# Attention weights of two units of the second batch turned through DRAM by VectorE, first batch's sums of v on GpSimd

## The chip, the cores and the metric

The kernel runs on one core of a Trainium2 chip. In the profile the core's engines are PE (TensorE, matrix products and transposes by product), DVE (VectorE), ACT (ScalarE), POOL (GpSimd) and SP (SyncE, which here only issues DMA transfers, one after the other). The metric is the device time of one execution in microseconds (us). The profiled execution has a time of its own and a span, from its first to its last instruction; all times inside the program are counted from the span's start.

## The reference

Eight batches of eight heads are attended in two ways and added; the sum is the input of a two-layer network. Cut to what is computed:

```python
# q, k, v: 8 batches, 8 heads, 576 positions, 64 wide
q_d = q.reshape(B, H, 144, 4, D).mean(axis=3)      # same for k_d, v_d
out_d = softmax(scale * q_d @ k_d.T) @ v_d         # 144 pooled positions
out_up = np.repeat(out_d, 4, axis=2)
mask = np.abs(pos[:, None] - pos[None, :]) < 4
scores = np.where(mask, scale * q @ k.T, -1e9)     # 7 keys for a query
out_local = softmax(scores) @ v
x = (out_up + out_local)                           # 4608 tokens x 512
h = x @ w_in                                       # 512 x 2048
g = h * np.clip(h + 3, 0, 6) / 6
return g @ w_out                                   # 2048 x 512
```

## The kernel before

**The large products.** The network is computed over chunks of tokens: 512 in chunk 0, 256 in chunk 1, then 384 each. For 16 slices f of the inner width `gemm1` (L934) makes h in PSUM, ScalarE and VectorE gate it (L940, L944) and split it into a rounded high part (L948) and a remainder, its low half (L952), and `gemm2` (L986) adds the slice to the output. Each float32 product is three products of rounded halves. The weights come as raw words, one block per slice of w_in and of w_out (SP, L169), and each block is made into two halves by ScalarE (L180, L195, L201), VectorE (L185, L189) and VectorE or GpSimd (L205, the remainder). All this happens while chunk 0 is worked on; the halves then stay.

**Attention.** A unit is a pair of heads of one batch, so each batch has four (0 to 3). A unit has pooled q and k (L331 and L333 on GpSimd), pooled v (sums of four rows), pooled scores (`scores_d`, L428), their softmax (normalised in L492 with 432 columns), local scores in windows (L607 puts the mask in by a product, L615 the scores) and their softmax (L492 with 640 columns). The normalised weights have the queries on the partitions, and the products with v need the keys there, so the weights have to be turned.

There are two ways to turn them. Units of batches 0 and 1 (`alone = b < ALONE`, ALONE = 2) are turned by TensorE: `trans_d` (L501, two groups of three transposes) and `trans` (L638, three and two), each with a copy out of PSUM behind it. Units of later batches go by DRAM: SP writes the pooled weights out (`put_d`, L511 to L516) and reads them back in blocks of 32 by 32 (`get_d`, L522 and L527), the local ones the same (`put` L541, `get` L548), and VectorE turns each block (`turn_d` L536, `turn_l` L555). The pooled product is `pv_d` (L586; L589 for batch 0) in the first case and `pv_d4` (L570) in the second; the local product is `pv` (L656).

**Sums of v.** `ld4` (L362 for the first 512 rows, g = 0; L364 or L367 for the last 64, g = 1) loads v for pooling. `sum_pe` sums four rows on TensorE: for g = 0 by four products with the identity (L393), for g = 1 by one product with a matrix of ones (L391). `sum4` does it with one reduction on VectorE (L376) or two additions on GpSimd (L378, L379). Batch 0 uses `sum_pe` for both, batch 1 for g = 1, all others `sum4`.

**What sets the order.** Nothing is ordered by hand. Every piece of work is an `op` with an engine (or several to choose from), a cost in us, the ops it follows, the buffers it takes and frees, and for some a due time. The class `Plan` simulates the five engines with these costs and always starts the ready op with the earliest due time; the order that comes out is emitted, and each engine runs its instructions in that order. `need`, with SLACK by batch, sets the due time of a batch's units. In the time up to the first `gemm1` the planner also puts fillers on TensorE (`busy`, L1038, products of an identity without use), as many as fit in the gaps that it expects. The names of buffers in the orders below: `early`, `arena` and `rows` are places in SBUF, `a_`, `o_` and `h_` with a number are banks of PSUM, `pd_` and `pl_` are tensors in DRAM for pooled and local weights, `rawp_` is a raw weight block.

## Time and profile before

| | us |
|---|---|
| median of 3 runs | 946.02 (945.36 to 947.41) |
| profiled execution | 944.02 |
| its span | 942.2 |
| TensorE busy | 931.6 (99% of the span) |
| VectorE busy | 554.2 (59%) |
| ScalarE busy | 363.2 (39%) |
| GpSimd busy | 298.8 (32%) |

Busy is the time in which an engine works on an instruction; shares are means over a program whose first sixth (attention of the first batches, the weights, chunk 0) is unlike the rest. TensorE's granted clock is 1.00 throughout. A timeline row gives start, duration (us), engine, line, operation, result and operands with their partitions and columns, and the number of records; in brackets stands the idle time before it and what ended it. A row of groups gives busy time in us and mean nanoseconds, then idle time and what released it. A row of waits gives the engine and what it waited for, then the total, the number and the longest. A row of windows gives start and end, length, and busy time and records of PE, PEld (weight loads), DVE, ACT and POOL, then clock, DMA share and GB/s. Some float32 products show two records per instruction.

### The profile page before, as it was taken

Reading aid. Unit: us, or ns where it says so; the run is one execution under the profiler, and the core shown is the slowest. Engines: PE = TensorE matmul, PEld = TensorE weight load, DVE = VectorE, ACT = ScalarE, POOL = GpSimd, SP = SyncE. Lnnn points to the kernel's source line nnn. Section 1 sums busy time; section 2 is a strip of 40 time slices with the busy share of each in tenths; the row PEclk is TensorE's granted clock in tenths of the full one; section 3 lists DMA queues with packets and bytes.
Section 4 is the critical chain, followed back from the end, with each engine's and each line's share of the span. In section 5 each row is a group of like instructions: output and inputs, shape, how many; then the busy total and the mean of one; then the engine's idle time right before and its main releaser. Section 6 shows DMA issues by size and latency. Waiting matters only on the chain.

```text
span 942.2 us, 19819 instructions
## 1 busy us (share of the span) xinstructions
PE 931.6 (99%) x7567; PEld 808.5 (86%) x7567; DVE 554.2 (59%) x1045; ACT 363.2 (39%) x899; POOL 298.8 (32%) x386
## 2 busy tenths in 40 slices
PE   8999999999999999999999999999999999999997
PEld 5677778988889898889889888988988988998996
DVE  7888886477677566554456667555455654323322
ACT  5787755334333334333233333333233432221222
POOL 4345361244462334332325244225125320000000
PEclk9999999999999999999999999999999999999999
DMA  7999353355666565545135555645154520100101
GB/s 210 228 293 288 72 118 64 70 105 119 126 134 132 104 117 113 100 84 114 34 80 122 102 104 102 134 98 97 40 99 80 115 55 12 34 1 2 33 1 33
DMA packets 311758, 93.52 MB, mean 99 GB/s; under 512 B 251376, under 2 KB 297840, under 8 KB 311664
## 3 DMA queue, kind: packets, MB, share of 16 engines
q1 hardware_dynamic: 311376, 91.83, 43.8%
q8 instruction: 59, 0.97, 0.4%
q10 hardware_dynamic: 288, 0.43, 0.2%
q14 instruction: 35, 0.29, 0.1%
HBM read 69.60 MB, written 22.61 MB: 98 GB/s over the span
## 4 chain that ended last, share of the span: by engine, by line
PE 90%; SPq 4%; DMA 3%; DVE 1%; issue 1%; ACT 1%; POOL 0%; DVEq 0%; ACTq 0%
PE h L934 40%; PE o L986 39%; PE a L656 2%; PE a L615 2%; PE a L442 1%; PE a L986 1%; PE a L570 1%; SPq L311 1%; DMA rows<-in_k_dram 1%; DMA arena<-in_v_dram 1%; SPq L548 1%; PE a L428 1%; SPq L522 1%; SPq L527 1%; DMA arena<-in_q_dram 0%
## 5 line engine op out<-in xcount | busy, mean ns | idle before, releaser
L934 PE MATMUL h<-rounded,wp 128*128 128x384 f32 (+2 forms) x2240 | 420.1, 336 | 0.2 <-DVE arena L944 0.2
L986 PE MATMUL o<-wp,rounded 128*128 128x512 f32 x1680 | 408.1, 394 | 0.0
L934 PEld LDWEIGHTS h<-rounded,wp 128*128 128x128 f32 x2240 | 384.1, 188 | 15.1 <-issue 2.7
L986 PEld LDWEIGHTS o<-wp,rounded 128*128 128x128 f32 x1680 | 311.0, 188 | 66.1 <-issue 4.4
L940 ACT ACTIVATE arena<-h 128x384 f32<-128x384 f32 (+2 forms) x192 | 93.7, 490 | 365.6 <-PE h L934 364.7
L944 DVE SCALAR_TENSOR_TENSOR arena<-arena,h 128x384 f32<-128x384 f32 (+2 forms) x192 | 105.1, 547 | 183.0 <-ACT arena L940 181.8
L948 ACT CAST rounded<-arena 128x384 fp32r<-128x384 f32 (+2 forms) x192 | 98.2, 512 | 119.2 <-DVE arena L944 118.7
L952 DVE TENSOR_TENSOR rounded<-arena,rounded 128x384 fp32r<-128x384 f32 (+2 forms) x136 | 79.9, 588 | 78.3 <-PE o L986 42.9
L952 POOL TENSOR_TENSOR rounded<-arena,rounded 128x384 fp32r<-128x384 f32 (+2 forms) x56 | 62.5, 1118 | 156.3 <-ACT rounded L948 102.9
L331 POOL TENSOR_TENSOR arena<-arena 128x144 f32<-128x144 f32 x36 | 16.2, 450 | 182.6 <-PE a L442 101.5
L318 DVE STREAM_TRANSPOSE arena<-arena 128x576 f32<-128x576 f32 x56 | 43.1, 772 | 24.1 <-PE a L615 11.4
L492 POOL TENSOR_TENSOR arena<-arena 128x640 f32<-128x640 f32 (+1 forms) x34 | 41.7, 1227 | 20.0 <-DVE arena L485 15.9
L333 POOL TENSOR_TENSOR arena<-arena 128x144 f32<-128x144 f32 x72 | 41.1, 570 | 5.6
L837 POOL TENSOR_TENSOR rounded<-arena,rounded 128x384 fp32r<-128x384 f32 (+1 forms) x10 | 15.0, 1511 | 71.2 <-ACT rounded L120 70.9
L473 POOL TENSOR_TENSOR arena<-arena 128x640 f32<-128x640 f32 x21 | 26.5, 1264 | 27.7 <-DVE arena L470 17.1
L376 DVE TENSOR_REDUCE arena<-arena 128x128 f32<-128x512 f32 (+1 forms) x28 | 30.0, 1071 | 8.8 <-PE a L570 6.9
L463 ACT ACTIVATE arena<-a,arena 128x144 f32<-128x144 f32 x84 | 31.5, 379 | 1.7
L536 DVE STREAM_TRANSPOSE arena<-arena 128x384 f32<-128x384 f32 (+1 forms) x48 | 21.5, 462 | 16.9 <-DMA arena<-pd 15.0
L205 POOL TENSOR_TENSOR wp<-early,wp 128x1024 fp32r<-128x1024 f32 (+1 forms) x9 | 19.4, 2158 | 34.4 <-ACT wp L201 34.4
L615 PE MATMUL a<-arena 64*64 64x64 f32 x1220 | 30.0, 223 | 0.0
L470 DVE TENSOR_REDUCE arena<-a 128x1 f32<-128x144 f32 (+2 forms) x65 | 26.1, 410 | 4.6 <-PE a L615 2.9
L656 PEld LDWEIGHTS a<-arena 64*64 64x64 f32 x1120 | 19.1, 134 | 9.5 <-issue 7.9
(186 smaller groups left out, 808.9 us busy)
## 6 DMA issues: line engine op xcount, KB each, us to landing
rawp<-in_w_in_dram SPq DMA_DIRECT2D x16, 512.0 KB
rawp<-in_w_out_dram SPq DMA_DIRECT2D x16, 512.0 KB
arena<-in_q_dram SPq DMA_DIRECT2D x112, 72.0 KB
arena<-in_k_dram SPq DMA_DIRECT2D x112, 72.0 KB
pl<-arena SPq DMA_DIRECT2D x24, 320.0 KB
arena<-pl SPq DMA_DIRECT2D x96, 80.0 KB
arena<-in_v_dram SPq DMA_DIRECT2D x28, 256.0 KB
out_dram<-arena SPq DMA_DIRECT2D x91, 72.0 KB
```

The source lines that it names most:

```text
L318: nc.vector.transpose(out=qk[kind], in_=st["raw", kind].rearrange("p j i -> p (j i)"))
L333: eng.tensor_tensor(t, t, x[:, :, r], op=ALU.add)
L463: nc.scalar.activation(p[:, j], x[:, j], AF.Exp, bias=m[:, j:j + 1], scale=1.0 / 128.0, accum_out=s[:, j:j + 1])
L492: eng.tensor_tensor(x, x, s.unsqueeze(2).broadcast_to(list(x.shape)), op=ALU.mult)
L615: nc.tensor.matmul(st["ps", g][half:half + WIN, jj * D:jj * D + WIN], qk_of("q")[hs, k_first:k_first + WIN], qk_of("k")[hs, k_first:k_firs ...
L656: nc.tensor.matmul(st["px"][g][h * D:(h + 1) * D, at + lo:at + hi], st["v"][ks, jj, h * D:(h + 1) * D], st["pt"][ks, jj, half + lo:half + ...
L934: nc.tensor.matmul(st["ps"], win[f][:, wt, kk * P:(kk + 1) * P], xs[part][:, kk], start=(kk == 0 and i == 0), stop=(kk == NK - 1 and i == ...
L940: nc.scalar.activation(st["t"], st["ps"], AF.Relu, bias=3.0)
L944: nc.vector.scalar_tensor_tensor(out=t, in0=t, scalar=6.0, in1=st["ps"], op0=ALU.min, op1=ALU.mult)
L948: nc.scalar.copy(st["gh"], st["t"])
L952: eng.tensor_tensor(st["gl"], st["t"], st["gh"].bitcast(F32), op=ALU.subtract)
L986: nc.tensor.matmul(otile[n, m], gt[:, ms], wout[f][:, wt], start=(f == 0 and i == 0), stop=(f == NF - 1 and i == 2),)
```

## The change

There are three parts. First, `turns(b, hp)` now decides how a unit's weights are turned, and it is true for batches from 2 on and for units 2 and 3 of batch 1 (`BOUNCED = 2, 3`): these two units go by DRAM and VectorE, use `pv_d4`, and have both sums of v by `sum4`. Their scores stay as they were. The buffer for the blocks read back (`rl1`) lies in room that a buffer of the weights' preparation (`zs`) loses. Second, the g = 0 sums of all four units of batch 0 go to GpSimd (`SUMMED = 0, 1, 2, 3`). Third, the planner's costs for TensorE's transposes, sums and small products in batches 0 and 1 are set to longer values, the due time of batch 1 moves (SLACK from 40 to 32), and the loop that opens units lets bounced units overlap as those of later batches do.

```diff
...
-                    a = early_user(op("PE", 0.33, tr, [l], take=[(PS, key), ("qkd" + k0, hk)], free=[rk], lag=LAGT, rec=3))
+                    a = early_user(op("PE", 0.66, tr, [l], take=[(PS, key), ("qkd" + k0, hk)], free=[rk], lag=LAGT, rec=3))
...
-            if b < ALONE or len(units) > 1:
+            if not turns(b, 2 * d + u) or (b, 2 * d + u) == (ALONE - 1, NHP - 1):
+                while units:
+                    next(units.pop(0), None)
+            elif len(units) > 1:
...
+        by_dram = turns(b, hp)
+        rl = "rl1" if alone else "rl"
...
-            elif alone:
+            elif not by_dram:
...
-            l = op("SP", 0.5, partial(ld4, g), take=[rk], size=dma(P, 512) if alone and g else dma((P, NAR)[g], 2048), nd=1 if alone else 1 + g)
+            l = op("SP", 0.5, partial(ld4, g), take=[rk], size=dma(P, 512) if not by_dram and g else dma((P, NAR)[g], 2048), nd=1 + g if by_dram else 1)
...
-            if b == 0 or alone and g:
+            if direct and (g or hp not in SUMMED) or not by_dram and not direct and g:
...
-                a = early_user(op("PE", 0.21 if g else 0.86, partial(sum_pe, g), [l], take=[bk], free=[rk], lag=LAGT, rec=2 if g else 8))
+                a = early_user(op("PE", (0.32 if direct else 0.52) if g else 0.92, partial(sum_pe, g), [l], take=[bk], free=[rk], lag=LAGT, rec=2 if g else 8))
...
-                sums.append(op(on("sum4", 1.0), 0, partial(sum4, g), [l], take=[("vd" + k0, un)], free=[rk]))
+                sums.append(op({"POOL": on("sum4", 1.0)["POOL"]} if direct else on("sum4", 1.0), 0, partial(sum4, g), [l], take=[("vd" + k0, un)], free=[rk]))
...
+                first, step = (h * D, 2 * D) if alone else (h * 3 * D, D)
...
-                    bass.AP(tensor=st["dd"].tensor, offset=st["dd"].offset + h * 3 * D * SD, ap=[[SD, D], [D * SD, 3], [1, SD]]),
+                    bass.AP(tensor=st["dd"].tensor, offset=st["dd"].offset + first * SD, ap=[[SD, D], [step * SD, 3], [1, SD]]),
...
-            st["rl"] = raw = buf("rl", un, [P, 20, NAR])
+            st["rl"] = raw = buf(rl, un, [P, 20, NAR])
...
-            nc.scalar.activation(st["od"], st["pod"] if alone else st["pod"][0], AF.Copy, scale=0.25)
+            nc.scalar.activation(st["od"], st["pod"][0] if by_dram else st["pod"], AF.Copy, scale=0.25)
...
-            sl_op = early_user(op("PE", 1.2, scores_l, turned["q"] + turned["k"] + masked, take=bks + [pl, sl], lag=LAGT, rec=42))
+            sl_op = early_user(op("PE", 1.3, scores_l, turned["q"] + turned["k"] + masked, take=bks + [pl, sl], lag=LAGT, rec=42))
...
-        if not alone:
+        if by_dram:
...
-        if alone:
+        if not by_dram:
...
-                    "PE", 0.3, partial(trans_d, g), [softmax_d], take=[tk_d, bk], free=[pk],
+                    "PE", 0.65 if direct else 0.76, partial(trans_d, g), [softmax_d], take=[tk_d, bk], free=[pk],
...
-                a = op("PE", 0.64, pv_d, evs_d + sums, take=[bk, ok], free=[tk_d, ("vd" + k0, un)], lag=LAGT, rec=8)
+                a = op("PE", 1.0, pv_d, evs_d + sums, take=[bk, ok], free=[tk_d, ("vd" + k0, un)], lag=LAGT, rec=8)
...
-                a = early_user(op("PE", 0.4 - 0.1 * i, partial(trans, i), [softmax], take=[tk, bk], free=[pl], lag=LAGT, rec=3 - i))
+                a = early_user(op("PE", (0.65 if direct else 0.76) - 0.2 * i, partial(trans, i), [softmax], take=[tk, bk], free=[pl], lag=LAGT, rec=3 - i))
...
-            a = op("SP", 2.0, get, [back_l], take=[("rl", un)], size=dma(20 * P, 128), nd=4)
-            t = [op("DVE", 0.8, turn_l, [a], take=[tk], free=[("rl", un)])]
+            a = op("SP", 2.0, get, [back_l], take=[(rl, un)], size=dma(20 * P, 128), nd=4)
+            t = [op("DVE", 0.8, turn_l, [a], take=[tk], free=[(rl, un)])]
...
-        if alone:
-            a = early_user(op("PE", 1.0, pv, t + lv + done_d, take=[] if direct else bks + xbs, free=[tk, vk], lag=LAGT, rec=40))
+        if not by_dram:
+            a = early_user(op("PE", 0.75 if direct else 1.0, pv, t + lv + done_d, take=[] if direct else bks + xbs, free=[tk, vk], lag=LAGT, rec=40))
...
-            dl = start_of(n) + TF * (f - two) * share + 0.01 * two
+            dl = start_of(n) + (TF if n else TF0) * (f - two) * share + 0.01 * two
...
-            dl = start_of(n) + TF * (f - two + LAG + (1.0 if n else 0.5)) * share + 0.01 * two
+            dl = start_of(n) + (TF if n else TF0) * (f - two + LAG + (1.0 if n else 0.5)) * share + 0.01 * two
...
-UNIT_T, EARLY, SLACK = (4.0, 22.0, 20.0, 30.0), 0.7, (4.0, 40.0, -5.0, 28.0)
...
+TF0 = 5.1
+UNIT_T, EARLY, SLACK = (4.0, 22.0, 20.0, 30.0), 0.7, (4.0, 32.0, -5.0, 28.0)
...
+BOUNCED = 2, 3
...
+SUMMED = 0, 1, 2, 3
...
-    assert t0 + 3 * big + NHP * (S - TOK0) * 4 <= slots["raw"][0][0]
+    tail = NHP * (S - TOK0) * 4
+    assert t0 + 2 * big + NWIN * D * 4 + tail <= slots["raw"][0][0]
...
-        "xb1": slots["xb"][1:], "lo": [(0, NK * big)], "x0": [(t0 + i * big, big) for i in range(3)],
-        "tail": [(t0 + 3 * big, NHP * (S - TOK0) * 4)],
+        "xb1": slots["xb"][1:], "lo": [(0, NK * big)],
+        "tail": [(slots["raw"][0][0] - tail, tail)], "rl1": [(t0 + 2 * big, NWIN * D * 4)],
...
-        "zf0": ["a0", "a1", "a2", "o0", "o1", "o2"], "zs": [(t0 + 2 * big, big)] + slots["raw"],
+        "zf0": ["a0", "a1", "a2", "o0", "o1", "o2"], "zs": slots["raw"],
...
+def turns(b, hp):
...
+    return b >= ALONE or b == ALONE - 1 and hp in BOUNCED
...
```

The rest of the change follows from the planner. Its orders are shown at three places. Lines are those of the changed kernel in the second block of each pair, 6 or 7 higher than before.

TensorE before, behind the two pooled scores of units 0 and 1 of batch 0 and the local scores of unit 1; L428 is a pooled score, L393 the g = 0 sum, L607 the mask of local scores:

```order
L428 MATMUL o_285<-early 64x144 x6
L393 MATMUL o_295<-early,ident 128x128 x4
L428 MATMUL a_307<-early 64x144 x6
L607 LDWEIGHTS identb
L607 MATMUL o_318<-maskb,identb 128x320
```

TensorE at the same place in the change, L434 being the pooled score, L397 the g = 1 sum, L1045 a filler and L614 the mask:

```order
L434 MATMUL o_258<-early 64x144 x6
L397 MATMUL o_269<-early,four 16x128
L434 MATMUL a_277<-early 64x144 x6
L397 MATMUL a_288<-early,four 16x128
L397 MATMUL o_291<-early,four 16x128
L1045 LDWEIGHTS identb
L1045 MATMUL h_99<-identb 128x512
L1045 LDWEIGHTS identb
L1045 MATMUL h_99<-identb 128x512
L614 LDWEIGHTS identb
L614 MATMUL a_302<-maskb,identb 128x320
```

The g = 0 sum is gone, three g = 1 sums follow the pooled scores at once, and the local scores that stood ahead of this place (unit 0's, between the transposes of the first and the second half) now stand behind the transposes of the second half.

GpSimd before, from its third pooled tensor on (L331 and L333 one pooled q or k, L492 a normalisation, L482 a small scaling):

```order
L331 TENSOR_TENSOR early<-arena 128x144
L333 TENSOR_TENSOR early<-early,arena 128x144 x2
L331 TENSOR_TENSOR early<-arena 128x144
L333 TENSOR_TENSOR early<-early,arena 128x144 x2
L492 TENSOR_TENSOR early<-early,arena 128x432
L482 TENSOR_SCALAR arena<-arena 128x10
L492 TENSOR_TENSOR arena<-arena 128x640
```

GpSimd in the change, from the same tensor on (L337 and L339 one pooled tensor, L384 and L385 a sum of v, L498 a normalisation):

```order
L337 TENSOR_TENSOR early<-arena 128x144
L339 TENSOR_TENSOR early<-early,arena 128x144 x2
L384 TENSOR_TENSOR early<-early 128x256
L385 TENSOR_TENSOR arena<-early 128x128
L337 TENSOR_TENSOR early<-arena 128x144
L339 TENSOR_TENSOR early<-early,arena 128x144 x2
L384 TENSOR_TENSOR early<-early 128x256
L385 TENSOR_TENSOR early<-early 128x128
L384 TENSOR_TENSOR early<-early 128x256
L385 TENSOR_TENSOR early<-early 128x128
L498 TENSOR_TENSOR arena<-arena 128x432
L384 TENSOR_TENSOR early<-early 128x256
```

The first sum stands ahead of the fourth pooled tensor, and the others stand ahead of and between the first normalisations.

SP before, in the loads of batch 2, where the last weight blocks stand:

```order
L355 DMA arena<-in_v_dram 64x128
L311 DMA arena<-in_q_dram 32x18x32 x4
L169 DMA rawp_1665<-in_w_out_dram 128x1024
L169 DMA rawp_1676<-in_w_out_dram 128x1024
L169 DMA rawp_1680<-in_w_out_dram 128x1024
L311 DMA arena<-in_k_dram 32x18x32 x4
```

SP in the change, at the bounce of unit 3 and up to the last weight blocks (L521 put_d, L529 and L534 get_d, L548 put, L555 get):

```order
L521 DMA pd_3_1495<-arena 64x3x144 x2
L555 DMA arena<-pl_2_1471 32x20x32 x4
L529 DMA arena<-pd_3_1495 32x12x32 x4
L534 DMA arena<-pd_3_1495 32x3x16 x4
L548 DMA pl_3_1591<-arena 128x5x128
L357 DMA arena<-in_v_dram 64x5x128
L555 DMA arena<-pl_3_1591 32x20x32 x4
...
L169 DMA rawp_1703<-in_w_out_dram 128x1024
L169 DMA rawp_1706<-in_w_out_dram 128x1024
L169 DMA rawp_1708<-in_w_out_dram 128x1024
```

The last three weight loads stand behind the bounce of unit 3 in SP's queue.

## The prediction

> **What bounds the kernel now.** I read the first part of the page, then what TensorE (PE) waited for over the whole span, then the busy times of all engines while the first chunk of the second part (30 to 155 us) is worked on.
>
> ```profile
> span 942.2 us, 19819 instructions
> PE 931.6 (99%) x7567; PEld 808.5 (86%) x7567; DVE 554.2 (59%) x1045; ACT 363.2 (39%) x899; POOL 298.8 (32%) x386
> ...
> PE h L1038 <- DVE identb L145: 2.9, 1, 2.9
> PE o L274 <- DMA arena<-in_k_dram: 1.1, 1, 1.1
> PE o L274 <- DMA rows<-in_k_dram: 0.6, 1, 0.6
> PE o L638 <- DVE arena L122: 0.4, 1, 0.4
> ...
> 30.00:155.00 125.00, 124.21 (x1085) 92.07 (x1084) 107.94 (x171) 90.23 (x175) 55.20 (x49) 1.00 0.68 187
> ```
>
> TensorE is busy for 931.6 of 942.2 us. Its four largest waits, all in the first 38 us (the first row is the start of the kernel), come to 5.0 us. So nothing that makes another engine faster can bring more than those. A gain here is TensorE work that disappears, and a loss is a wait of TensorE that is new. The last row shows the engine that could make such waits: VectorE (third number, 107.94 of 125.00) has only 17.1 us free in that stretch.
>
> **A: the sums of the first batch.** The four units' 128x128 sums of v, four matmul instructions each (two records each), leave TensorE:
>
> ```profile
> L393 PE MATMUL o<-early,ident 128*128 128x128 f32 x16 | 2.2, 281 | 0.0
> L393 PE MATMUL a<-early,ident 128*128 128x128 f32 x16 | 2.1, 275 | 0.0
> ```
>
> That is 4.3 us of records. Neighbouring records overlap by some 0.1 us a group (the 0.39 us record at 95.11 below occupies the 0.32 us until 95.43), so the slots come to 3.6 to 4.3; I take 3.9.
>
> **B: fillers.** The order of the change holds 9 of the fillers (matmuls without use that keep TensorE running) instead of 19.
>
> ```profile
> L1038 PE MATMUL h<-identb 128*128 128x512 bf16 x19 | 5.8, 432 | 2.9 <-DVE identb L145 2.9
> 2.90 1.89 PE L1038 MATMUL h<-identb 128*128 128x512 bf16 x4 [2.90 <-DVE identb L145]
> ```
>
> The first four (1.89 us) stay. The other 15 take (5.8 - 1.89)/15 = 0.26 each, ten are 2.6. They sit where the planner thought there would be a gap; if a gap is really there, their time comes back as a wait. That is counted in D, so B is 0 to 2.6 on its own.
>
> **C: units 2 and 3 of the second batch.** Each loses its small sum (L391), its transposes of the pooled weights (L501) and of the local ones (L638), and the pooled product of its own (L586). The slot of each is the start of the next row less its own:
>
> ```profile
> 95.11 0.39 PE L391 MATMUL a<-arena,four 64*16 64x128 f32 x2
> 95.43 0.95 PE L428 MATMUL a<-arena 64*64 64x144 f32 x12
> ...
> 105.86 0.82 PE L501 MATMUL a<-ident,arena 128*128 128x128 f32 x6
> 106.43 0.48 PE L934 MATMUL h<-rounded,wp 128*128 128x512 f32 x1
> ...
> 109.34 0.86 PE L586 MATMUL a<-arena 128*64 128x144 f32 x8
> 110.13 2.35 PE L986 MATMUL o<-wp,rounded 128*128 128x512 f32 x9
> ...
> 113.01 0.71 PE L638 MATMUL a<-ident,arena 128*128 128x128 f32 x5
> 113.48 0.48 PE L934 MATMUL h<-rounded,wp 128*128 128x512 f32 x1
> ...
> L570 PE MATMUL a<-arena 64*64 64x144 f32 x288 | 16.0, 285 | 0.0
> ```
>
> 0.32 + 0.57 + 0.79 + 0.47 = 2.15 us a unit. In their place stands the pooled product of the other path, 16.0 us in 24 units = 0.67. So 2.15 - 0.67 = 1.48, and for two units 3.0. Everything else of TensorE keeps its count. **A + B + C = 9.5 us** if TensorE stays dense.
>
> **D: what comes back in the first 38 us.**
>
> ```profile
> 10.13 0.43 PE L607 MATMUL a<-maskb,identb 128*128 128x320 bf16 x2
> ...
> 11.24 0.55 PE L274 MATMUL a<-ident,rows 128*128 128x128 f32 x3
> ...
> 13.01 0.52 PE L274 MATMUL o<-ident,rows 128*128 128x128 f32 x3 [0.57 <-DMA rows<-in_k_dram]
> ...
> 19.14 0.91 POOL L492 TENSOR_TENSOR early<-early,arena 128x432 f32<-128x432 f32 x1 [1.55 <-DVE arena L485]
> ...
> 58.66 0.75 POOL L378 TENSOR_TENSOR arena<-arena 128x256 f32<-128x256 f32 x1
> 59.48 0.46 POOL L379 TENSOR_TENSOR arena<-arena 128x128 f32<-128x128 f32 x1
> ...
> 34.20 1.05 DVE L376 TENSOR_REDUCE arena<-arena 128x128 f32<-128x512 f32 x1
> ...
> 18.07 0.49 SPq L364 DMA_DIRECT2D early<-in_v_dram  x1
> ...
> 183.20 0.40 SPq L541 DMA_DIRECT2D pl<-arena  x1
> ...
> 185.86 1.97 SPq L548 DMA_DIRECT2D arena<-pl  x4
> ```
>
> D1: the local scores of unit 0 stand at 10.13 to 11.24 and so cover 1.11 us of the wait for the second half's k rows, which land at 13.01 whatever TensorE does. In the new order they stand behind those transposes, and one filler ahead of them is gone too. The wait grows from 0.57 to about 1.8, so 1.2 to 1.3 of A to C is lost there. This is read from rows that do not change, and I hold it the surest of the three.
>
> D2: GpSimd's first sum (0.75 + 0.46 = 1.21, from the two rows at 58.66) now stands ahead of its products of pooled q and k for the last half. TensorE had some 0.7 us of slack to these, so about 0.5 is lost. The small sum of unit 2 now stands right behind, but its rows are issued at 18.07, and an issue of 0.49 with a landing after it of about 2.2 (the write issued at 183.20 to 183.60 let its read go at 185.86) means 20.8; TensorE would be there about 19.8: another 1.0.
>
> D3: GpSimd has a sum (1.21) of another unit ahead of unit 1's normalisation (0.91, row at 19.14), and that sum waits for its own load, which lands about 23.4 by the same rule. So unit 1's weights are ready at 23.4 + 1.21 + 0.91 = 25.5; TensorE would start to turn them about 24.4 by the rows from 14.11 us on, set in the new order. With the transposes behind it 1.1 to 1.3 are lost. The 0.43 of the wait at L638 goes, since VectorE's copy has more time.
>
> D is 1.25 + 1.5 + 1.3 - 0.43 = 3.6. If GpSimd's sums find their loads landed early, only D1 less 0.43 stays: 0.8. If each of the other sums also meets a late load, about 6. I take 3.6, built from the rows nearest to each place.
>
> [...] This trace shows GpSimd's two adds at 1.21 against VectorE's one reduction of 1.05 for the same sum, a ratio of 1.15. [...]
>
> **E: VectorE in chunk 0.** The two bounced units give VectorE their turns, the planner moved normalisations and low halves onto it, and took two weight remainders and two sums off it.
>
> ```profile
> L555 DVE STREAM_TRANSPOSE arena<-arena 128x640 f32<-128x640 f32 x24 | 20.1, 839 | 10.9 <-DMA arena<-pl 10.9
> L492 DVE TENSOR_TENSOR arena<-arena 128x432 f32<-128x432 f32 x19 | 12.3, 647 | 0.7
> 132.54 1.39 SPq L169 DMA_DIRECT2D rawp<-in_w_out_dram  x3
> ...
> 98.08 1.22 DVE L205 TENSOR_TENSOR wp<-early,wp 128x1024 fp32r<-128x1024 f32 x1
> 153.61 0.69 DVE L205 TENSOR_TENSOR wp<-arena,wp 128x512 fp32r<-128x512 f32 x1
> ...
> 158.76 2.23 PE L986 MATMUL o<-wp,rounded 128*128 128x512 f32 x9
> ```
>
> Ahead of the last weight it gains two times about 1.65 of turns (0.84 for the local part, about as much for the pooled part), three normalisations of 640 columns (0.647 x 640/432 = 0.96 each) and one of 432, together 3.5, and four low halves of 512 columns at about 0.69 (2.8); it loses 2 x 1.22 and 2 x 1.05. That is +5.0 us. The last weight is done at 154.3 and used at 158.8, so 4.5 us of slack. VectorE's free 17.1 us are mostly waits for TensorE, which shrink as TensorE comes earlier. If TensorE comes 4 to 5 us earlier at the end of chunk 0 and VectorE 5 us later, it must fill some 10 of its 17 free us with no loss. I expect most of it to fit and 1.4 us of waits to be left: between 0 (all of it fits) and 6 (none). On SP's queue each bounced unit adds a put (0.40) and four reads (1.97) for the local weights and ten issues for the pooled ones, at 0.4 to 0.5 each, so 7 us of issuing. The loads of the last three w_out blocks, issued at 132.54 before, now stand behind the whole bounce of unit 3 in SP's queue, which waits in order. From their issue to 154.3 there were 21.8 us, so some 10 us of delay are hidden; more would add to E, and unit 3's bounce should be over by 130.
>
> **Sum.** 9.5 - 3.6 - 1.4 = 4.5 us. The span goes from 942.2 to 937.7, the profiled execution from 944.0 to 939.5. The median of the runs before, 946.0, is 2.0 above that execution, so I predict 941.5.
>
> **Rivals.** R1, TensorE stays nearly dense: D only 0.8, E nothing. A planner with measured durations may well have put the moved sums where their loads are in time, though the order in D1 speaks against a full gain. 9.5 - 0.8 = 8.7: 937.3.
>
> R2, VectorE becomes the bound of chunk 0. If its free time cannot be filled, the last weight is not ready 4 us earlier but 5.0 + 0.8 us later than 154.3, at 160.1, 1.3 after the use of before; TensorE's work behind that place is 3.0 less for what has been moved ahead of it. -3.0 + 1.3 = -1.7: 944.3. For it speaks the 86% of VectorE in 30 to 155; against it that these waits are on TensorE for the most part.
>
> R3, the turned weights come late, and the kernel gets slower. Between a unit's scores and its products TensorE now has only what the order puts between: for unit 3 of the second batch 72 matmuls of the two large products, 72 x 2.23/9 = 17.8 us. Behind the waiting product stand all the large products of chunk 0's end, and their results release the rest. How long such a chain lasts is seen in later batches, from the local scores to the end of the last turn:
>
> ```profile
> 169.19 0.75 PE L615 MATMUL a<-arena 64*64 64x64 f32 x36
> ...
> 192.31 0.83 DVE L555 STREAM_TRANSPOSE arena<-arena 128x640 f32<-128x640 f32 x1
> ...
> 209.18 0.75 PE L615 MATMUL a<-arena 64*64 64x64 f32 x36
> ...
> 236.93 0.85 DVE L555 STREAM_TRANSPOSE arena<-arena 128x640 f32<-128x640 f32 x1 [0.41 <-DMA arena<-pl]
> ```
>
> 193.1 - 169.2 = 23.9 less 0.75 of scores is 23.2; 237.8 - 209.2 = 28.6 less 0.75 is 27.9. Against 17.8 that would be a wait of 5.4 or 10.1. Those chains had time to spare, with TensorE long busy elsewhere, and are no lower bound: without the queues of SP and VectorE the pieces come to some 14 or 15 us. But in chunk 0 VectorE is fuller than there. With 27.9 and D, E left as they are but for E's 1.4: -9.5 + 3.6 + 10.1 = +4.2: 950.2. It decides from a chain of about 23.7 us on (a wait of 5.9 uses up the gain) and is told as slower from about 25.6.
>
> [...]
>
> **Chances.** The forecast (TensorE's work goes, about half is given back at the front and in chunk 0) 0.52; R1 0.16; R2 0.18; R3 0.14. A change of 0.2%, 1.9 us, is about what a measurement here tells from none. Of the forecast nine in ten are faster by more than that (0.47), of R1 all (0.16), of R2, which lies just within, two fifths (0.07): faster 0.70. Within: 0.05 + 0.11 = 0.16. R3 is slower: 0.14. The forecast's own range is 939 to 944 (D 1.5 to 5, E 0 to 3). For 8 in 10 it must take in half of R1, down to 936.5, and the part of R3 with chains up to about 26 us, up to 948.
>
> **What would show it.** A to C: no 128x128 group of sums on TensorE, 9 fillers, 17.3 us in the pooled products of the second path. D1: the wait of TensorE for the k rows near 13 us at about 1.8 instead of 0.6. D2, D3: new waits for GpSimd and for a v load between 18 and 27 us, some 3 us together. E: new waits of a large product for VectorE's L205 remainder or low halves, below 3 us in all. R3 would be one wait of several us of the second batch's product for a VectorE turn at 110 to 150 us. I am wrong if TensorE's busy time falls by less than 8 us, or if the sum of its new waits is above 8 or below 2.

## The result and the profile after

The changed kernel is slower: 957.34 us (median of 4 runs, 953.93 to 963.84) beside 945.69 for the kernel before, a ratio of 1.0133 (1.0107 to 1.0158). The forecast was 941.5 with a range up to 948.0. The runs of the changed kernel scatter over ten us, those of before over two. A ratio leaves out runs that are more than 1.5% above the fastest of the same kernel, which here are two of the seven runs of e5 below (962.11 and 964.20). The profiled execution is the fastest of the four: 953.93, with a span of 952.1.

The head of the changed kernel's page:

```profile
span 952.1 us, 19750 instructions
PE 927.8 (97%) x7507; PEld 804.1 (84%) x7507; DVE 568.1 (60%) x1056; ACT 357.0 (37%) x883; POOL 310.3 (33%) x404
```

What TensorE waited for (total, times, longest):

```profile
PE h L941 <- DVE arena L951: 6.5, 4, 4.0
PE h L1045 <- DVE identb L145: 2.9, 1, 2.9
PE a L397 <- DMA arena<-in_v_dram: 1.9, 1, 1.9
PE o L397 <- DMA early<-in_v_dram: 1.5, 1, 1.5
PE o L274 <- DMA rows<-in_k_dram: 1.2, 1, 1.2
PE a L274 <- DVE early L333: 1.2, 1, 1.2
PE a L663 <- issue: 1.1, 1, 1.1
PE o L993 <- DVE wp L205: 0.9, 1, 0.9
PE a L434 <- POOL early L339: 0.6, 1, 0.6
```

The busy times of all engines in the stretch shown of the kernel before, and the two stretches at half clock (the third number from the end is the granted clock):

```profile
30.00:155.00 125.00, 120.52 (x1059) 89.34 (x1058) 112.70 (x174) 84.53 (x160) 66.32 (x61) 0.97 0.74 196
...
37.50:44.00 6.50, 6.50 (x61) 3.29 (x59) 2.95 (x9) 2.75 (x8) 1.30 (x2) 0.50 1.03 410
262.70:266.00 3.30, 3.30 (x11) 3.30 (x12) 1.32 (x3) 0.84 (x2) 0.00 (x0) 0.50 0.75 191
```

Before, the waits came to 5.6 us and the granted clock was 1.00. Now they come to 19.3 us, VectorE has 12.3 us free in that stretch instead of 17.1, and in two places the clock is halved (37.40 to 44.23 and 262.68 to 266.09 us). TensorE's timeline at the two, with a row of the second kind at full clock ahead of it:

```profile
35.88 0.38 PE L397 MATMUL a<-arena,four 64*16 64x128 f32 x2 [1.85 <-DMA arena<-in_v_dram]
36.93 3.90 PE L596 MATMUL o<-early 128*64 128x288 f32 x16
...
248.71 4.35 PE L941 MATMUL h<-rounded,wp 128*128 128x384 f32 x24
...
262.58 5.99 PE L941 MATMUL h<-rounded,wp 128*128 128x384 f32 x24 [4.00 <-DVE arena L951]
```

Both follow a wait. The pooled product of the first kind in the kernel before:

```profile
40.25 2.32 PE L589 MATMUL o<-early 128*64 128x288 f32 x16
```

Its sixteen records took 2.32 us there and take 3.90 here; a pair of slices (24 records) takes 4.35 at full clock and 5.99 behind the 4.00 us wait. Of the 5.99 us 3.4 were at half clock; counted half they leave 2.6 + 1.7 = 4.3, as at full clock. At half clock 6.8 us and 3.4 us were worked, so 5.1 us are lost to the clock.

The account of the span, where work is span less waits, less half of the time at half clock, less the 5.0 us that are left, 4.8 of them at the end, when TensorE is done:

| us | before | after | difference |
|---|---|---|---|
| work of TensorE at full clock | 931.6 | 922.7 | -8.9 |
| its waits | 5.6 | 19.3 | +13.7 |
| lost at half clock | 0 | 5.1 | +5.1 |
| end of the execution, gaps below 0.15 | 5.0 | 5.0 | 0 |
| span | 942.2 | 952.1 | +9.9 |

So the work did fall by what the change takes off. The waits have three places: 5.7 us more in the first 38 us, 3.2 more from there to the end of chunk 0, and 4.9 after it (1.22 at 199.8, 4.00 at 262.6, less 0.36 in the kernel before).

### The profile page after: what moved, and what is told of

It is laid out like the page before. It is cut to its first block, busy times and chain, and to the rows that moved or that the text cites. A ratio compares the mean times of both kernels' runs of the same rounds, so it can differ in the third digit from the quotient of the medians.

```text
span 952.1 us, 19750 instructions
## 1 busy us (share of the span) xinstructions
PE 927.8 (97%) x7507; PEld 804.1 (84%) x7507; DVE 568.1 (60%) x1056; ACT 357.0 (37%) x883; POOL 310.3 (33%) x404
## 4 chain that ended last, share of the span: by engine, by line
PE 88%; DVE 4%; SPq 3%; DMA 3%; issue 1%; POOL 0%; ACT 0%; DVEq 0%
PE h L941 40%; PE o L993 39%; PE a L663 2%; PE a L622 2%; PE a L448 1%; PE a L577 1%; DMA early<-in_v_dram 1%; DMA arena<-in_k_dram 1%; SPq L317 1%; PE a L993 1%; PE o L596 1%; DMA arena<-in_v_dram 1%; SPq L357 0%; DVE arena L389 0%; DVE arena L324 0%
## 5 line engine op out<-in xcount | busy, mean ns | idle before, releaser
L951 DVE SCALAR_TENSOR_TENSOR arena<-arena,h 128x384 f32<-128x384 f32 (+2 forms) x192 | 104.7, 547 | 183.2 <-ACT arena L947 182.5
L959 DVE TENSOR_TENSOR rounded<-arena,rounded 128x384 fp32r<-128x384 f32 (+2 forms) x145 | 85.2, 589 | 78.4 <-PE o L993 44.6
L959 POOL TENSOR_TENSOR rounded<-arena,rounded 128x384 fp32r<-128x384 f32 (+2 forms) x47 | 51.3, 1091 | 115.7 <-ACT rounded L955 84.5
L337 POOL TENSOR_TENSOR arena<-arena 128x144 f32<-128x144 f32 x37 | 17.0, 458 | 190.8 <-PE a L448 114.2
L339 POOL TENSOR_TENSOR arena<-arena 128x144 f32<-128x144 f32 x74 | 42.4, 573 | 5.8
L844 POOL TENSOR_TENSOR rounded<-arena,rounded 128x768 fp32r<-128x768 f32 (+2 forms) x15 | 20.6, 1389 | 71.8 <-ACT rounded L120 71.0
L498 POOL TENSOR_TENSOR arena<-arena 128x640 f32<-128x640 f32 (+1 forms) x29 | 34.7, 1197 | 13.3 <-DVE arena L491 9.7
L205 POOL TENSOR_TENSOR wp<-early,wp 128x1024 fp32r<-128x1024 f32 (+1 forms) x11 | 24.3, 2213 | 35.4 <-ACT wp L201 16.4
L663 PEld LDWEIGHTS a<-arena 64*64 64x64 f32 x1120 | 18.9, 134 | 10.2 <-issue 9.2
L622 PEld LDWEIGHTS a<-arena 64*64 64x64 f32 x1200 | 25.6, 134 | 2.1 <-issue 2.1
```

Source lines behind the costliest of these rows:

```text
L339: eng.tensor_tensor(t, t, x[:, :, r], op=ALU.add)
L498: eng.tensor_tensor(x, x, s.unsqueeze(2).broadcast_to(list(x.shape)), op=ALU.mult)
L622: nc.tensor.matmul(st["ps", g][half:half + WIN, jj * D:jj * D + WIN], qk_of("q")[hs, k_first:k_first + WIN], qk_of("k")[hs, k_first:k_firs ...
L663: nc.tensor.matmul(st["px"][g][h * D:(h + 1) * D, at + lo:at + hi], st["v"][ks, jj, h * D:(h + 1) * D], st["pt"][ks, jj, half + lo:half + ...
L951: nc.vector.scalar_tensor_tensor(out=t, in0=t, scalar=6.0, in1=st["ps"], op0=ALU.min, op1=ALU.mult)
L959: eng.tensor_tensor(st["gl"], st["t"], st["gh"].bitcast(F32), op=ALU.subtract)
```

## The experiments

Theory G: waits of TensorE set the clock down, and the fillers that the new costs leave out would have held it. Theory V: the later waits come from the place of a few instructions in VectorE's order. Theory B: the bounce brings the later waits. Theory P: the planner's order of before is a good one among many, and any new order brings waits of its own, whatever the changed work is worth. Other letters are explained in the expectation that uses them. In the diffs of experiments that keep an order and move parts of it, an op has the planner's number: MORE adds fillers ahead of an op, MOVES puts ops ahead of another one.

| label | kernel | median us | ratio to before (95%) |
|---|---|---|---|
| e1_fill | changed, 23 fillers in the front's waits | 953.32 | 1.0107 (1.0066 to 1.0148) |
| e2_no_bounce | changed, no bounce | 950.82 | 1.0066 (1.0035 to 1.0097) |
| e3_no_sums | changed, sums on TensorE | 953.93 | 1.0108 (1.0075 to 1.0140) |
| e4_costs_only | changed, no bounce, no sums: the new costs alone | 951.93 | 1.0071 (1.0050 to 1.0092) |
| e5_gates | changed, three gates moved | 953.05 | 1.0050 (1.0024 to 1.0076) |
| e6_fill16 | changed, 16 fillers at one place | 953.44 | 1.0077 (1.0055 to 1.0098) |
| e7_old_costs | changed, old costs | 948.62 | 1.0029 (1.0013 to 1.0045) |
| e8_bounce_only | changed, old costs, no sums: the bounce alone | 956.20 | 1.0110 (1.0089 to 1.0130) |
| e9_before_no_fillers | before, 15 fillers less | 945.48 | 1.0005 (0.9991 to 1.0020) |
| e10_old_costs_mended | e7, three pieces moved | 944.63 | 0.9998 (0.9989 to 1.0007) |
| e11_due_time_only | before, one due time | 951.11 | 1.0055 (1.0035 to 1.0074) |
| e12_transposes_cost | before, one cost | 955.26 | 1.0110 (1.0088 to 1.0132) |
| e13_mended_twice | e10, more pieces moved | 945.20 | 1.0003 (0.9993 to 1.0014) |

### Fillers where TensorE waits

```diff
+MORE = {91: 4, 98: 4, 148: 2, 111: 5, 79: 1, 163: 1, 475: 6}
```

> The changed kernel with 23 more fillers of about 0.26 us, put where TensorE waits in the first 36 us (4 before each of the two groups of transposes that wait 1.2 us, 2, 5, 1 and 1 before the waits at 18.6, 21.3, 25.7 and 29.2 us, 6 before the small sum of the second batch that waits 1.85 us until 35.9). Nothing else moves. [...] Rival W (only the waits count): the granted clock still drops or its drop does not matter, the fillers only take the place of idle time, and the time is the same or up to 1 us longer.

953.3, 4 less than the changed kernel's median (957.3), though the span of the profile is 0.5 longer. The waits in the first 30 us shrank, but the one at the second batch's small sum grew from 1.85 to 2.51 us, since there TensorE waited for a copy by ScalarE, which itself stood still 2.6 us for a weight's load. Behind it the clock was halved again, for 3.4 us instead of 6.8. By G the time would be some 951 to 952, the profiled 953.93 less 2 to 3 of the 3.4 us lost at half clock from 37.40 to 44.23. It is above that, and neither G nor W is settled by this run.

```diff
+MORE = {475: 16}
```

> The changed kernel with 16 fillers, 4.2 us, at one place only: ahead of the second batch's small sum, where TensorE waits 1.85 us and behind which the clock is halved for 6.7 us. Theory G: the wait is covered whole, the clock stays at 1.00 between 37 and 44 us, so 3.4 us come back, and the 2 us or so that the fillers take beyond the wait are lost; the span falls by 1 to 2 us, to about 950.5, and the clock's mean is 0.998. Rival W: the clock is halved there all the same and the span rises by 2.

With 16 fillers at that one place the wait there is gone and the clock is whole from 20 to 50 us. But in this execution an earlier wait of 2.24 us for rows of q, up to 11.55 us, is followed by a halving, as the windows show:

```profile
10.00:15.00 5.00, 2.62 (x16) 2.44 (x17) 3.27 (x5) 0.53 (x1) 1.76 (x5) 0.80 0.93 190
15.00:20.00 5.00, 5.00 (x58) 3.72 (x60) 2.87 (x5) 2.89 (x12) 4.61 (x9) 0.52 0.67 190
20.00:30.00 10.00, 9.29 (x205) 6.16 (x194) 9.48 (x27) 7.61 (x30) 6.38 (x11) 1.00 0.95 212
30.00:40.00 10.00, 9.61 (x95) 5.03 (x95) 7.66 (x16) 6.11 (x15) 7.54 (x12) 1.00 0.90 287
40.00:50.00 10.00, 10.00 (x140) 5.55 (x141) 8.46 (x20) 8.32 (x17) 2.55 (x2) 1.00 1.01 313
```

In this profile the clock is whole behind the covered wait, as G says. But the fillers take about what that saves, another wait set the clock down elsewhere, and neither the expected 950.5 nor the mean clock of 0.998 was reached (0.992 to 0.997 in the four runs).

```diff
-            if o.busy:
+            if o.busy and o is order[[x.eng for x in order].index('PE')]:
                 busy(o.busy)
```

> The kernel before with 15 of its 19 fillers left out (the first four, at the kernel's start, stay), all else word for word. TensorE's work falls by 15 x 0.26 = 3.9 us, and idle time stands where the fillers were. Theory G (the fillers hold the clock up): the gaps at 9 to 10, 20 to 22, 30 to 31 and 38 us grow to 1 to 2 us, the clock is halved for some us behind one or more of them as it was in the changed kernel, and the time is 2 to 6 us above before, with a clock of 0.99 to 0.997 and more scatter. Rival W (a filler takes only time that TensorE would wait anyway, or less): clock 1.00 and the time within 1 us of before or up to 3 us below.

945.48: no difference, so the 2 to 6 us that G gave are refuted. The head of its page, the largest waits of TensorE besides the start, and two windows:

```profile
span 942.9 us, 19789 instructions
PE 930.6 (99%) x7552; PEld 808.9 (86%) x7552; DVE 557.7 (59%) x1045; ACT 363.0 (39%) x899; POOL 297.5 (32%) x386
```

```profile
PE o L501 <- POOL arena L492: 1.2, 1, 1.2
PE a L615 <- DVE arena L122: 0.8, 1, 0.8
PE o L274 <- DMA rows<-in_k_dram: 0.7, 1, 0.7
```

```profile
30.00:40.00 10.00, 8.88 (x94) 4.85 (x93) 8.79 (x18) 5.95 (x14) 5.19 (x7) 0.92 0.95 344
40.00:50.00 10.00, 10.00 (x168) 6.50 (x170) 7.46 (x16) 7.05 (x16) 1.59 (x2) 0.91 0.88 180
```

No wait is above 1.2 us, and still the clock is halved once, from 38.41 to 41.82 us, around two waits of 0.57 and 0.55 us where two fillers had stood. So in this execution 2.7 us of work at full clock are gone (busy 930.6 less 1.7 at half clock, beside 931.6), and 1.9 us come back as waits and 1.7 as half clock. The mean clock is 1.000 in three of the ten runs (943.49 to 945.38 us) and 0.992 in one (950.32). That fits G, by which fillers can hold the clock, but in sum they are worth nothing here, and so are ten fillers less.

### The three parts, one undone or one alone

```diff
-BOUNCED = 2, 3
+BOUNCED = ()
```

> The changed kernel with no bounced unit (units 2 and 3 of the second batch turned by TensorE again); the sums on GpSimd and the planner's new costs stay. TensorE has 3.0 us more work. Theory B (the bounce brings the late waits at 145 to 157, 199.8 and 262.6 us, 2.1 + 1.2 + 4.0 with 1.7 of half clock, through VectorE's added work): these are gone and the time falls by about 6, to 948. Rival P (the waits come from any new order that the planner makes): waits of some us for VectorE stand at other places and the time rises by up to 3.

950.8, with runs from 945.96 (clock 0.998) to 958.40 (0.981). In the profile, of the fastest run, TensorE waits for nothing after 67.3 us: the waits at 145 to 157, 199.8 and 262.6 are gone, as B says (by the median the time falls by 6.5 us, about the 6 that B gave). What is left is the front, where the small sum of the second batch waits 2.65 us with the clock halved behind it.

```diff
-SUMMED = 0, 1, 2, 3
+SUMMED = ()
```

> The changed kernel with the first batch's sums of v back on TensorE (four products each); bounce and new costs stay. TensorE has 3.9 us more work. Theory S (GpSimd's sums and the small sums behind them make the front's waits): the waits between 18 and 30 us, 0.64 + 1.48 + 0.51 + 0.28, go, the front's end comes at the same time, and the total is within 1 us plus what the clock gives back, 951 to 954. Rival (the sums are a gain that other waits hide): the waits stay and the time rises by about 4 to 958.

953.9; the profile is of the longest of the four runs (959.61). The waits for GpSimd and v loads at 18 to 26 us are gone, but others stand at 39.7 and 43.5 (0.93 and 2.97, for copies) and at 161.8 and 164.6 (3.58 and 2.21, for the halves of chunk 1's x). The part about the front held, and the total is what was expected for another reason.

Edited against the changed kernel:

```diff
-BOUNCED = 2, 3
+BOUNCED = ()
...
-SUMMED = 0, 1, 2, 3
+SUMMED = ()
```

> The kernel before with only the planner's new costs and due time for the second batch (and the changed places of some buffers): no bounced unit, no sum on GpSimd. TensorE's work is that of before less 8 fillers, 2.1 us. Theory F (longer costs leave too few fillers and put waits in their place): new waits in the front of more than 2 us, a granted clock below 1, and the time is above before, 948 to 952. Rival (the costs are a better picture of TensorE): the time is 1 to 2 us below before, 944.

951.9, as theory F of its expectation has it: more than half of the loss is there with no unit bounced and no sum moved. Waits of 1.78 (for a copy by ScalarE, at 29.5), 1.26 and 0.95 at 40 us are new, and the clock is 0.66 from 40 to 50 us and halved once more, from 70.8 to 74.2. (Of the new costs one is shorter, not longer: the first batch's local product, from 1.0 to 0.75.)

Edited against the changed kernel; the other six costs go back in the same way:

```diff
-                    a = early_user(op("PE", 0.66, tr, [l], take=[(PS, key), ("qkd" + k0, hk)], free=[rk], lag=LAGT, rec=3))
+                    a = early_user(op("PE", 0.33, tr, [l], take=[(PS, key), ("qkd" + k0, hk)], free=[rk], lag=LAGT, rec=3))
...
-UNIT_T, EARLY, SLACK = (4.0, 22.0, 20.0, 30.0), 0.7, (4.0, 32.0, -5.0, 28.0)
+UNIT_T, EARLY, SLACK = (4.0, 22.0, 20.0, 30.0), 0.7, (4.0, 40.0, -5.0, 28.0)
```

> The changed kernel with the planner's costs and due time of before: bounce and sums on GpSimd stay, and the planner puts 26 fillers in. Theory F (the new costs make the planner leave TensorE idle without fillers, so the clock falls): with old costs the clock in the front stays at 1.00, and TensorE works 4.4 us longer on fillers; the time is below the changed kernel's by 2 to 6 us, 948 to 952. Rival (the waits of bounce and sums set the clock off anyway): granted clock and time as in the changed kernel, 954 or more.

948.6, 9 us less than with the new costs and within what F gives. F's mechanism did not come with it: the clock in the front is not whole, but halved for 3.4 us behind a wait of 1.54 (at 24.9) and again behind one of 1.90 (at 62.3). The waits at 199.8 and 262.6 are not there, although the bounce is: B cannot be their whole cause.

Edited against the changed kernel, with all old costs as in e7:

```diff
-                    a = early_user(op("PE", 0.66, tr, [l], take=[(PS, key), ("qkd" + k0, hk)], free=[rk], lag=LAGT, rec=3))
+                    a = early_user(op("PE", 0.33, tr, [l], take=[(PS, key), ("qkd" + k0, hk)], free=[rk], lag=LAGT, rec=3))
...
-UNIT_T, EARLY, SLACK = (4.0, 22.0, 20.0, 30.0), 0.7, (4.0, 32.0, -5.0, 28.0)
+UNIT_T, EARLY, SLACK = (4.0, 22.0, 20.0, 30.0), 0.7, (4.0, 40.0, -5.0, 28.0)
...
-SUMMED = 0, 1, 2, 3
+SUMMED = ()
```

> The kernel before with only the bounce of units 2 and 3 of the second batch; costs and the first batch's sums as before, 19 fillers. TensorE's work falls by 3.0 us. Theory B (the bounce by itself brings late gates and products through VectorE): new waits for VectorE of some us after 100 us, and the time is 2 to 5 us above before, 948 to 950. Rival (the bounce alone is the gain that was meant): its 3 us come through and the time is 942 to 943.

956.2, worse than both expected, and 7.6 us worse than e7, which differs in the sums alone. Here the weights are late, which is R2 of the prediction, and gates again. What TensorE waited for:

```profile
PE h L941 <- DVE arena L951: 5.2, 3, 3.8
...
PE o L993 <- ACT wp L201: 2.7, 1, 2.7
PE o L993 <- POOL wp L205: 1.6, 1, 1.6
PE o L993 <- DVE wp L205: 0.8, 1, 0.8
```

The weight waits end at 139.6, 142.1 and 154.8 us. VectorE worked without a gap from 132.4 on, and the steps of these weights stand there (134.5 to 139.1) behind sums of v and a gate. The last three loads, behind the bounce in SP's queue, were issued at 142.8 instead of 132.5; they can explain the third wait at most, and that was not tried apart.

### Single instructions moved

In the changed kernel the 4.00 us wait reads like this on VectorE:

```profile
256.23 0.78 DVE L324 STREAM_TRANSPOSE arena<-arena 128x576 f32<-128x576 f32 x1 [2.09 <-DMA arena<-in_k_dram]
256.93 0.24 DVE L491 RECIPROCAL arena<-arena 128x3 f32<-128x3 f32 x2
257.08 1.03 DVE L382 TENSOR_REDUCE arena<-arena 128x128 f32<-128x512 f32 x1
...
258.24 1.02 DVE L382 TENSOR_REDUCE arena<-arena 32x128 f32<-32x512 f32 x1
259.30 1.71 DVE L389 TENSOR_SCALAR arena<-arena,head 32x64 f32<-32x64 f32 x2
...
261.99 1.01 DVE L951 SCALAR_TENSOR_TENSOR arena<-arena,h 128x384 f32<-128x384 f32 x2
```

The gates (L951), which empty the banks that TensorE needs, stand behind the turn of a k that waits for its load, and behind sums of a later unit.

```diff
+MOVES = [([689], 919), ([780, 784, 785], 1038)]
```

> The changed kernel with three of VectorE's gate instructions (L951) set ahead of the work of later units that stands before them in its order: one at 199.4 us ahead of a pooled sum, the product scaling and a v sum, two at 262.0 us ahead of the turn of a k that waits for its load until 256.2 and of two v sums. TensorE's order is untouched. Theory V (these two waits of TensorE, 1.22 and 4.00 us, and 1.7 us of half clock behind the second, come from VectorE's place in the order alone): both waits go, the clock stays 1.00 at 262 to 266, and the span falls by 5 to 7 us to about 946. Rival (VectorE has no room there, the work put back is late in its turn): waits of the same sum come up behind, and the span falls by less than 2.

Both waits are gone; 1.50 at 211.6 (for a low half) and 1.85 at 286.9 come up, with a halving behind the latter. The profile is of the run of 962.11, in which the clock is halved from 37.90 to 61.79 us, so it serves here only for the places of the waits. TensorE comes to the second place some 10 us later in it; but the load of k lands 11 us later (its turn starts at 267.10), and the gates now stand ahead of it, at 265.40. So V holds for these two waits. The ratio falls from 1.0133 to 1.0050, some 8 us, and the median over all runs from 957.34 to 953.05, 4 us. The 8 is an upper end, since the changed kernel's own run of 963.84 stays in its ratio.

```diff
+MOVES = [([146, 147], 48), ([352, 353], 507), ([631], 314)]
```

> The changed kernel with the old costs (bounce and sums on GpSimd stay; before this 948.6), with three pieces of its order moved: the fourth small sum of batch 0, which waits 1.54 us for its load with a halved clock behind it, goes behind four transposes and a set of scores; the first gate (and its relu) goes ahead of two pooled tensors on VectorE, where TensorE waits 1.90 us with a halved clock behind it; one low half of chunk 1's x goes ahead of a weight's step on VectorE, where TensorE waits 1.67. Theory V/G (the waits that are left, and the clock behind two of them, come from the places of few instructions, and the work taken off TensorE is worth its 9 us less fillers): the three waits shrink by about 4, the two halvings (3.4 us together) go, and the time is 941 to 943.5, below the kernel before. Rival P (waits come back at other places as soon as these go): 947 to 949.

944.6, 4.0 below the same kernel without the moves, and equal to the kernel before. It lies between V's 941 to 943.5 and P's 947 to 949. The two halvings, 3.4 us together, are gone; the waits fell only from 11.2 to 10.3.

```diff
+MOVES = [([146, 147], 48), ([352], 227), ([353], 509), ([630, 631], 878),
+         ([317], 322), ([33], 109), ([68], 144)]
```

> The mended kernel with old costs and four more pieces moved: two normalisations of the first batch go ahead of two sums on GpSimd (TensorE waits 1.20 for the first), the first gate and its relu go further ahead (0.88), a high and a low half of chunk 1's x go ahead of the turn of a k on VectorE (1.07), and a weight's remainder one step ahead (0.73). Theory V: these four waits of 3.9 shrink by 2 to 3 and the time is 941.5 to 943, 0.2 to 0.4% below before. Rival P: they come back at other places and the time stays at 944 to 945.

945.2: rival P. Of the four waits that were to go (3.9 us), two shrank (0.88 to 0.71, 0.73 to 0.62 in two pieces), one became 0.70 at the next transposes, one stayed (1.06), and new ones of 0.72, 0.32 and 0.27 came. The head of its page and TensorE's largest waits but the start:

```profile
span 943.0 us, 19783 instructions
PE 928.1 (98%) x7524; PEld 803.1 (85%) x7524; DVE 563.2 (60%) x1055; ACT 360.1 (38%) x888; POOL 308.1 (33%) x397
```

```profile
PE h L941 <- DVE arena L951: 1.4, 2, 0.7
PE h L941 <- DVE rounded L844: 1.1, 1, 1.1
PE o L274 <- DMA rows<-in_k_dram: 0.8, 1, 0.8
PE a L507 <- DVE early L479: 0.7, 1, 0.7
```

With the clock whole, TensorE works 3.5 us less than before and waits 4.0 us more. No version that beats the kernel before was found.

### A new order without new work

```diff
-UNIT_T, EARLY, SLACK = (4.0, 22.0, 20.0, 30.0), 0.7, (4.0, 40.0, -5.0, 28.0)
+UNIT_T, EARLY, SLACK = (4.0, 22.0, 20.0, 30.0), 0.7, (4.0, 32.0, -5.0, 28.0)
```

> The kernel before with one number changed, the due time of the second batch (SLACK from 40 to 32), which is one piece of the change's third part. Every instruction stays what it was; the planner's order differs in some hundred rows of TensorE and of VectorE, and 15 fillers stand instead of 19. Theory P (the order of before is a good one among many, and any new order brings waits of its own): new waits of 2 to 5 us at other places and a time of 948 to 951. Rival (only the changed operations cost something): the time is within 1 us of before.

951.1, at the upper end of P's range. In the profile, of the longest of the four runs (954.05), there are new waits of 2.54, 1.07, 0.56 and 0.56 us at 154 to 161 us, and the clock is halved from 156.8 to 167.0. It is also halved from 13.4 to 16.8 us, behind waits of 0.59 and 1.30, and from 37.3 to 40.7, where no wait stands:

```profile
20.00:30.00 10.00, 9.98 (x148) 6.99 (x146) 8.79 (x26) 7.40 (x30) 5.56 (x8) 1.00 0.90 211
30.00:40.00 10.00, 10.00 (x100) 6.48 (x100) 7.99 (x18) 5.27 (x11) 5.60 (x8) 0.87 0.93 298
40.00:50.00 10.00, 10.00 (x169) 5.80 (x168) 8.71 (x18) 8.91 (x18) 1.62 (x2) 0.96 0.98 243
```

The profile shows no wait of TensorE from 13.3 us on up to this halving; the work just ahead of it, from 32.7 to 37.3, is pooled products of the first batch (L589).

```diff
-                    a = early_user(op("PE", 0.33, tr, [l], ...
+                    a = early_user(op("PE", 0.66, tr, [l], ...
```

> The kernel before with one cost changed, that of the first batch's q and k transposes (0.33 to 0.66), another piece of the third part. Same instructions, 11 fillers, a new order of the front. Theory P: waits of 2 to 5 us more than before, most of them in the front, a granted clock below 1 behind the longest, and a time of 948 to 952, as with all new costs together (951.9). Rival (this cost is not where the loss of the new costs comes from): within 1 us of before.

955.3, above the range given, and the waits are not in the front but at 65 to 75 us. TensorE's two largest but the start, and the windows there:

```profile
PE a L638 <- POOL arena L492: 3.5, 1, 3.5
...
PE o L986 <- DVE wp L205: 2.4, 1, 2.4
```

```profile
60.00:70.00 10.00, 5.38 (x60) 3.77 (x60) 6.11 (x9) 6.00 (x10) 4.90 (x2) 0.75 1.01 224
70.00:80.00 10.00, 7.63 (x66) 5.59 (x63) 8.37 (x14) 8.55 (x19) 4.39 (x3) 0.57 0.70 223
```

Both kernels do the work of before but for 4 and 8 fillers, which e9 shows to be worth nothing in sum; the planner also put 6 more pieces on VectorE (1051 instead of 1045) and as many less on ScalarE and GpSimd together. One planner number costs 5.7 and 9.8 us, half and more than four fifths of the 11.7 of the whole change. P holds for both new orders tried: without any changed work a new order can cost nearly as much as the change did.

## Why the prediction was wrong

The span was forecast at 937.7 and came out at 952.1. To within rounding the 14.4 us between them are 0.6 less work removed, 2.1 more in D, 1.8 more in E, 4.9 of waits behind chunk 0 and 5.1 of half clock; for the last two the sum had no term. Both of the prediction's own signs of being wrong came: TensorE's busy time fell by 3.8 us only, since half clock lengthens it by 5.1, and its waits grew by 13.7.

**The sum of removed work (A, B, C) was right in size and wrong in worth.** 9.5 us were forecast and 8.9 left TensorE. But B, 2.6, was no gain: 15 fillers less change the time by nothing in e9. B had been given as 0 to 2.6 with its lower end tied to D; the upper end was taken in the sum.

**D was the right place and too small:** 3.6 forecast, 5.7 measured, inside its bounds of 0.8 to 6. D1 was 1.21 + 1.23 less the 0.57 of before, 1.9 instead of 1.25: the k rows landed at 12.96, as read, and their wait was 1.23 instead of 1.8, but ahead of it stands a new one of 1.21 for VectorE. D2 was 0.64 + 1.48 = 2.1 instead of 1.5. D3 was 0.51 + 0.28 = 0.8 instead of 1.3. GpSimd's sums took 1.2 us (0.73 + 0.46 at 15.6 us), as read from the trace of before. The 0.43 went, as forecast, and the first wait for a load fell from 1.07 to 0.57. Not seen was the small sum of the second batch, which now stands ahead of the first large products and waits 1.85 us.

**E was mis-sized, and its carrier was wrong.** 1.4 forecast, 3.2 measured. The last weight's remainder did come later, at 162.5 instead of 154.3, but TensorE did not wait for it. It waited for the bounced weights' turn and then for gates and the halves of chunk 1's x (1.10, 0.88, 0.15), and earlier for one weight and a gate (0.92 and 0.39).

**The step that failed most is "everything else of TensorE keeps its count", taken as "keeps its time".** The places searched for waits ended with chunk 0. Two waits behind it, 1.22 and 4.00, come from VectorE's order, which the planner changed everywhere and which the prediction did not look at there. No kernel without the bounce has them, but they are not its price as such: e3 and e7 have the bounce without them, e8 has them again, and moving three gates takes them off (e5).

**The clock has no term in the sum and costs 5.1 us in the profiled run, and more in the other three by their mean clock (0.981 to 0.992 beside 0.995).** Before, no wait but the start was longer than 1.1 us, and the granted clock was 1.00 in every stretch. The prediction's own D and E forecast waits of that size and above, and the row that would have priced them could not be in the trace of before. By the 15 profiles, the start left out, 12 of 13 waits of 2 us and more that began at full clock brought a halving, which in five cases began before the wait had ended (none came of the one of 3.06 up to 263.3 us in e6), and so did 4 of 11 between 1.5 and 2.0 us. Seven halvings have no wait of 1.5 us ahead of them: some stand behind one wait of 1.1 to 1.3 us or several short ones close together (e4 at 70 us: 0.35, 0.54 and 0.80), and the one of e11 at 37.3 us behind none. So waits explain most of the clock's falls and not all. The halvings of the profiled run lasted 6.83 and 3.41 us; the first began at 37.40, 1.52 us after a wait of 1.85, and the second at 262.68, 0.10 us after the wait of 4.00.

**The rivals.** R1 is refuted. R2, VectorE as the bound through weights, shows in e8 and in the change only with one wait of 0.92. R3 has its wait, for the turn of unit 3, but it is 1.10 us and not 5 to 10: from the end of its local scores (126.10) to the end of the turn (145.13) the chain took 19.0 us, where R3 needed 23.7. The time went slower, as R3 had it, by another mechanism. What no rival held is P: that the order of before, against which each removed piece was counted, is itself worth 5.7 and 9.8 us over the two others that were tried without the change's work.

Undone one by one the parts do not add up (costs alone 6.7 us, bounce alone 10.8, all three 11.7 over their own runs of before), since each makes an order of its own. The sums alone were not run. How much of the 11.7 is due to each part stays open in that sense. What is shown: with bounce and sums kept and the old costs, 8.7 us less, and with three pieces moved, 12.7 less.

## What to carry to other kernels

Where a planner makes the order, a change of its costs is a change of the whole program: compare the new orders by their waits in every stage, and run a control in which one planner number moves and no work does, before any gain is put down to the work. Where TensorE is busy for 99% of the span, ask of each piece of work taken off it whether something else was about to arrive at its place: here 15 fillers taken out of a front that waits for loads brought nothing (e9), and 3.9 us of sums put back there cost nothing (e3). In these kernels a new wait of 2 us or more cost itself and, in 12 of 13 cases, brought a halving of 3.4 us or more.

## What the hardware showed

A halving of the clock was seen behind single waits of 1.1 to 4.0 us, behind several shorter ones, and once with no wait ahead of it (e11, 37.3 us). In the clock records of the 15 traces there are 23 halvings while TensorE works. They last 3.41 us (14 of them), 6.83 (6), 10.24, 13.65 and 23.89, whole multiples of 3.41. Their starts lie such multiples apart as well: 66 in the changed kernel (37.40 and 262.68 us), 7 and 35 in e11 (13.4, 37.3 and 156.8). Why no halving followed the wait of 3.06 us in e6, where one came behind a wait of 1.54 us in e7, is not shown.

In the profile of e5 a halving lasted from 37.90 to 61.79 us although TensorE was busy for all of the 20 us from 40 to 60, at small products for the most part. Executions of the same program differ with the clock: ten runs without the bounce went from 945.96 at a mean clock of 0.998 to 958.40 at 0.981, and the kernel before, whose profile has no wait over 1.1 us but the start, stays within 5 us in each of four sets of 13 to 21 runs, at a mean clock of 0.997 to 1.000.
